# Dummy products in TensorE's wait for x, two small loads held back, and a new planned order, in a fused attention and state-space kernel

## The chip, the cores and the metric

One core of one Trainium2 chip runs the whole kernel as one program. The metric is the device time of one execution in microseconds; each version's number is the median of its runs.

## The reference

x is 2048 tokens of 448 features, bf16. Two branches read the same x, and a gate mixes them.

```python
x = A_x                                              # (1, 2048, 448)
g = sigmoid((x * gate_w).sum(-1, keepdims=True))
# A: attention, 16 heads of 28, one K and one V head for all
q = (x @ wq) as 16 heads;  k = x @ wk;  v = x @ wv
a = softmax(q k^T * 28**-0.5) v, heads joined, @ wo
# B: state-space convolution, 448 channels, 256 modes
dt = exp(log_dt);  logdA = dt * (A_re + i A_im);  dB = dt * (B_re + i B_im)
K[d, l] = Re sum_n C[d, n] exp(logdA[d, n] * l) dB[d, n]
b = causal convolution of x with K, over l, + x * Dskip
return g * a + (1 - g) * b
```

## The kernel before

Nobody writes the instruction order by hand. The kernel registers operations (`pg.op` for an engine, `pg.dma` for a load or store), each with what it reads and writes, an estimated duration and a priority; the planner (`Prog.schedule`) then simulates the five engines and fixes one order per engine. Lower (time, priority, number) goes first. Until the first exponential is planned, an operation on a longer remaining path to it can pass another; `RANK` adds nanoseconds to that path for single operations, named by their number. `LOW` is the share of a 3,413 ns stretch that TensorE should be busy: where the plan shows less, `idle` puts filler products (L1423, into P·V's bank, adding zeros) into a planned gap. `AHEAD` and `SLACK` shift when the planner takes a bank or a dependent operation for ready.

**The start.** SP issues the loads of x in four blocks of 512 tokens, in the order `QO` = 0, 3, 1, 2. Blocks 0 and 3 arrive as they are and TensorE transposes them in four parts T each (L718), from banks 0 and 1, copied to SBUF by ScalarE where the pair (block, T) is in `XA` (L728) and by VectorE else (L730). Blocks 1 and 2 come transposed by the DMA (L153, on SP's queue). Then four products per block make K (L736; block 2 in bank 5), VectorE takes the largest absolute value (L742), and K's copy to SBUF is VectorE's where the block is in `KD` (L746), else ScalarE's (L750). The first head's query follows: four products (L954), a maximum (L960), the bias weights (L768, L774, L775), a product that adds the bound (L963), the copy (L966). After that the first scores (L1337) and the first exponential (L1372) can run. V's and the gate's weights are loaded from GpSimd's queue (L632, L633) and copied by VectorE (L645, L647) for V's products (L763). Dummy products (`self.warm`, L554) on the identity are placed at several points here; the identity comes from GpSimd (L541, L542). ScalarE also prepares the state-space parameters, with three changes of its function table (the last, to exp, at L911).

**The middle.** 1024 score tiles of 128 keys by 512 queries are taken in sets of three and two. TensorE makes scores with 4 row-tiled products (L1337) or one over masked queries (L1347), ScalarE takes the exponential (L1372), TensorE multiplies with V (L1409). Beside that VectorE builds 14 groups of tables of powers (L1029 to L1075), TensorE turns them into kernels (L1095), GpSimd writes these to DRAM, SP loads them back as Toeplitz tiles (L1131), and TensorE convolves (L1155).

**The end.** The last heads are divided by their sums (`norm_last`: L1244, L1247, L1248), multiplied with wo (`outp`, L1198; L1265), added to the output with the gate (`fold`, L1207), while the last convolutions are scaled (L1170), turned (L1181) and added (L1189); then the stores.

Of the kernel before, what the change touches and what calls it, by code (L numbers as in the profile page):

```python
# [35 lines left out]
TW = 4 * 1024  # L36
XQ = NT * 512
SIN2PI = 6.2831850
XA = ((0, 1), (0, 3), (1, 0), (1, 1), (1, 2), (2, 3), (3, 0), (3, 1), (3, 2))
KD = (0, 2, 3)  # L40
GX = 3
DQ = (1, 2)
VNS = 140
# [41 lines left out]
class Prog:  # L85
# [6 lines left out]
    BLOCK, FIRST, FETCH, IDLE, NEED = 256, 192, 5900.0, 3300.0, .015  # L92
    HALF = (21000.0, 21000.0, 1.8)
    HEAD = 0.4
    RANK = {111: 3000, 190: -6000, 29: -6000, 38: -6000, 43: 3000, 23: -1500, 41: -3000, 192: -6000, 82: -1500, 153: -6000, 27: -3000, 118: 1500, 37: 1500, 150: -6000, 105: 3000, 39: -6000, 74: -1500, 92: 3000}
    POOL = (7,)
    LOW, SPAN, FILL = .45, 3413.0, (36000.0, 490000.0)
    AHEAD = 1500.0
    SLACK = {"pe": 700.0, "dve": 150.0}

    def __init__(self, nc, es):
        self.nc, self.es = nc, es
# [356 lines left out]
class Kernel:  # L459
# [131 lines left out]
    def loads(self):  # L591
# [37 lines left out]
        pg.dma(rows(wst, 0, ins["A_wq"], D), (448, 896), "wq", wr=["wqs"], cost=1500, extra=300)  # L629
        lx(QO[2])  # L630
        lx(QO[3])
        pg.dma(rows(wks, 4 * DH, ins["A_wv"], DH), (448, 56), "wv", wr=["wvs"], eng="pool", cost=150, extra=2500)  # L632
        pg.dma([(wks.v(0, P, 8 * DH, [[2, 3]]), dram(ins["gate_w"], 0, [[1, P], [P, 3]])),  # L633
                (wks.v(0, 64, 8 * DH + 6, [[1, 1]]), dram(ins["gate_w"], 384, [[1, 64], [1, 1]]))], (448, 2), "wg", wr=["wgs"], slow=True, eng="pool", cost=150, extra=2500)
# [67 lines left out]
    def prep_x(self):  # L702
        pg = self.pg
# [3 lines left out]
        for iq, q in enumerate(QO):  # L707
            xT, xo = self.xq(q)
            t4, o4 = self.bank((4, 3, 2, 5)[iq])
            X = ("b", (4, 3, 2, 5)[iq])  # L710
            for T in (2, 0, 3, 1) if q not in DQ else ():
                b = nb % 2
                nb += 1
                t, o = self.bank(b)

                def mm(e, q=q, T=T, t=t, o=o):
                    for k in range(4):
                        r = e.matmul(t.v(0, P, o + 128 * k, [[1, 128]]), xst.v(0, P, q * XP + k * D + 128 * T, [[1, P]]),  # L718
                                     self.ident.v(0, P, 0, [[1, P]]), start=True, stop=True, tile_position=(0, 0),
                                     skip_group_check=True)  # L720
                    return r
                pg.op("pe", mm, 415, rd=[("xst", q), "id"] + ["xp"] * (T == 3), wr=[("b", b)])
                last = len(pg.ops) - 1
                src = bass.AP(tensor=t.h, offset=o, ap=[[t.rs, P], [128, 4], [1, 2], [2, 64]])
                dst = xT.v(0, P, xo + T * 512, [[128, 4], [64, 2], [1, 64]])
                key = ("xT", T, q)
                if (q, T) in XA:
                    pg.op("act", lambda e, d=dst, s=src: e.activation(d, s, AF.Copy), 535, rd=[("b", b)], wr=[key])  # L728
                else:
                    pg.op("dve", lambda e, d=dst, s=src: e.tensor_copy(d, s), 600, rd=[("b", b)], wr=[key])  # L730

            for _ in range((2, 0, 0, 0)[iq]):
                pg.after[len(pg.ops)] = last
                self.warm(1, 5, 300)
            for n, T in enumerate((2, 0, 3, 1)):
                pg.op("pe", lambda e, n=n, T=T, t4=t4, o4=o4, xT=xT, xo=xo: e.matmul(  # L736
                    t4.v(0, P, o4, [[1, 512]]), self.Wk.v(0, P, T * P, [[1, P]]), xT.v(0, P, xo + T * 512, [[1, 512]]),
                    start=(n == 0), stop=(n == 3), tile_position=(0, 0), skip_group_check=True),
                    215, rd=["Wk", ("xT", T, q)], wr=[X])
                self.k3 = len(pg.ops) - 1  # L740
            kv, od = kT.v(0, P, 512 * q, [[1, 512]]), [[1, 512]]
            pg.op("dve", lambda e, q=iq, t4=t4, o4=o4: e.tensor_reduce(  # L742
                sm.v(0, P, 8 + q, [[1, 1]]), t4.v(0, P, o4, [[1, 512]]), AX.X, ALU.max, apply_absolute_value=True), 600,
                rd=[X], wr=[("km", iq)])
            if q in KD:
                pg.op("dve", lambda e, kv=kv, t4=t4, o4=o4, od=od: e.tensor_scalar(  # L746
                    kv, t4.v(0, P, o4, od), sm.v(0, P, 0, [[1, 1]]), None, ALU.add), 600,
                    rd=[X, "s0"], wr=[("kT", q)], pr=-2)
            else:
                pg.op("act", lambda e, kv=kv, t4=t4, o4=o4, od=od: e.activation(  # L750
                    kv, t4.v(0, P, o4, od), AF.Identity, bias=sm.v(0, P, 0, [[1, 1]])), 580,
                    rd=[X, "s0", ("km", iq)], wr=[("kT", q)], pr=-2)
            if q:
                o = pg.dma([(dram(self.XS, (q - 1) * P * XQ + o, [[XQ, n], [1, w]]), xT.v(0, n, xo + o, [[1, w]]))
                            for o, n, w in ((0, P, 1536), (1536, 64, 512))],
                       (128, 4096), f"xs{q}", rd=self.xk(q), wr=[("XS", q)], pr=0.3)
                self.lastxs = o.i
# [380 lines left out]
    def conv(self, c):  # L1138
# [29 lines left out]
        if c % 8 == 7 and c < 24:  # L1168
# [1 line left out]
        pg.op("dve", lambda e: e.tensor_tensor(self.cst.v(0, P, cs * 512, [[128, 4], [64, 2], [1, 64]]),  # L1170
                                               ps.v(0, P, 63, [[128, 4], [64, 2], [-1, 64]]),
                                               self.omq.v(0, P, 0, [[0, 4], [64, 2], [1, 64]]), ALU.mult),
              el(512), rd=[X, "omq"], wr=[("cst", cs), X], pr=(2, 2)[c > 25])
        Y = ("yx", c)

        def yt(e, k):
# [7 lines left out]
                                 start=(mu == 0), stop=(mu == 1), tile_position=(0, 64 * par), skip_group_check=True)  # L1184
            return r
        for k in range(4):
            pg.op("pe", lambda e, k=k: yt(e, k), 70, mode="h", ni=8, rd=[("cst", cs), "id"], wr=[Y], pr=1.55)
        ov = self.O.v(0, P, 15 * D + 16 * c, [[-D, 16], [1, 16]])
        pg.op("dve", lambda e: e.tensor_tensor(ov, ov, px.v(0, P, 0, [[1, 16], [16, 16]]), ALU.add),  # L1189
              el(256), rd=[Y], comm=tuple(("O" if c < 26 else "Oz", q) for q in range(7)), pr=(2, 0.5)[c > 25], unlock=px)  # L1190
# [1 line left out]
    def outp(self, qc, tt):  # L1192
        pg = self.pg
        X = ("ox", qc, tt)
        G = self.grp()
        px = lambda: G.v(0, P, 0, [[1, D]])
        for g in range(4):
            pg.op("pe", lambda e, g=g: e.matmul(  # L1198
                px(), self.onT.v(0, P, g * 512 + 128 * tt, [[1, 128]]), self.Wo.v(0, P, g * D, [[1, D]]),
                start=(g == 0), stop=(g == 3), tile_position=(0, 0), skip_group_check=True), 200,  # L1200
                rd=["Wo"] + [("on", gg) for gg in (0, 1, 2, 4 if (qc, tt) == (3, 2) else 3)], wr=[X], pr=1.2 if qc == 3 else 1.65, lock=G if g == 0 else None)
        self.fold(qc, tt, px, 0, D, [X], unlock=G)

    def fold(self, qc, tt, px, off, n, rd, unlock=None):
        tl = 4 * qc + tt
        ov = self.O.v(0, P, D * tl + off, [[1, n]])
        self.pg.op("dve", lambda e: e.scalar_tensor_tensor(ov, px(), self.gt.v(0, P, tl, [[1, 1]]), ov, ALU.mult, ALU.add),  # L1207
                   el(n), rd=rd + ["gt"], comm=(("O", qc + tt * (qc == 3)), ("Oz", qc + tt * (qc == 3))), pr=(2, 1.5)[qc == 3], unlock=unlock)

    def norm(self, i):  # L1210
        pg = self.pg
# [20 lines left out]
    def norm_last(self, i, o, n, bank, key):  # L1232
# [2 lines left out]
        hv, rv, on = w(self.acc, 512 * (i % 2)), w(self.rdenB, 0), w(self.onT, 512 * (i % 4))  # L1235
        ak = [("acc", i % 2, o) if o else ("acc", i % 2)]
        if bank is None:
            G, pe, dve = self.grp(), 0.9, 0.9
            bc, bk = lambda: G.v(0, P, 0, [[1, n]]), [("bx", i, o)]
        else:  # L1240
            G, pe, dve = None, 0, 0
# [45 lines left out]
    def main(self):  # L1287
# [36 lines left out]
        def qk(s):  # L1324
# [4 lines left out]
            def row(e):  # L1329
                for t, b in zip(ts, bs):  # L1330
                    if joint(t):
                        full(e, t, b, 1)
                for j in range(4):
                    for t, b in zip(ts, bs):
                        i, parts, qo, n = dec(t)
# [168 lines left out]
```

## Time and profile before

| what | value |
|---|---|
| runs, us | 504.24, 505.18, 506.43 (median 505.18) |
| profiled execution, us | 505.32 |
| its span, us | 503.5 |
| ScalarE busy | 480.7 us (95%) |
| VectorE busy | 456.9 us (91%) |
| TensorE busy (matmul) | 427.1 us (85%) |
| GpSimd busy | 169.7 us (34%) |
| DMA moved | 139.51 MB |

The span runs from the program's first to its last instruction; the execution's time adds what lies around it. Profile times are microseconds from the span's start. PE is TensorE's matmul part, PEld its weight loads, DVE is VectorE, ACT ScalarE, POOL GpSimd, and a "q" behind a name (SPq) stands for the sequencer that issues. In a line on a group of instructions, the numbers behind the bar are busy time and mean ns of one, then the idle time of the engine just ahead of them and what ended it. The granted clock is the share of TensorE's clock that the chip let through.

### The profile page before, as it was taken

Reading aid. Unit: us, or ns where it says so; the run is one execution under the profiler, and the core shown is the slowest. Engines: PE = TensorE matmul, PEld = TensorE weight load, DVE = VectorE, ACT = ScalarE, POOL = GpSimd, SP = SyncE. Lnnn points to the kernel's source line nnn. Section 1 sums busy time; section 2 is a strip of 40 time slices with the busy share of each in tenths; the row PEclk is TensorE's granted clock in tenths of the full one; section 3 lists DMA queues with packets and bytes.
Section 4 is the critical chain, followed back from the end, with each engine's and each line's share of the span. In section 5 each row is a group of like instructions: output and inputs, shape, how many; then the busy total and the mean of one; then the engine's idle time right before and its main releaser. Section 6 shows DMA issues by size and latency. Waiting matters only on the chain.

```text
span 503.5 us, 18673 instructions
## 1 busy us (share of the span) xinstructions
PE 427.1 (85%) x8288; PEld 190.9 (38%) x8395; DVE 456.9 (91%) x836; ACT 480.7 (95%) x430; POOL 169.7 (34%) x312
## 2 busy tenths in 40 slices
PE   5887878787797899779888899889888899899985
PEld 2322123242343434334443444344444444343543
DVE  7999999999999999999999999999999999923333
ACT  5899899999999999999999999999999999999971
POOL 8833223432143423414344421535042252514000
PEclk9899799999999999999999999999999999999989
DMA  8976921899959696999999989799997979799992
GB/s 189 218 209 124 60 35 44 280 292 350 328 186 306 225 349 211 285 367 329 354 318 364 336 303 366 210 357 378 356 364 249 369 256 387 242 347 365 385 343 47
DMA packets 122563, 139.51 MB, mean 277 GB/s; under 512 B 55321, under 2 KB 62538, under 8 KB 122482
## 3 DMA queue, kind: packets, MB, share of 16 engines
q1 hardware_dynamic: 112208, 128.89, 79.9%
q0 software_dynamic: 8784, 9.27, 6.9%
q8 instruction: 66, 1.08, 0.9%
q10 hardware_dynamic: 1490, 0.14, 0.2%
q14 instruction: 15, 0.12, 0.1%
HBM read 125.18 MB, written 5.22 MB: 259 GB/s over the span
## 4 chain that ended last, share of the span: by engine, by line
DVE 44%; ACT 42%; PE 10%; SPq 2%; issue 1%; DMA 1%; DVEq 0%
ACT expT L1372 42%; DVE tab L1048 7%; DVE tab L1059 4%; DVE tab L1060 4%; DVE tab L1070 3%; DVE tab L1057 3%; DVE tab L1058 3%; DVE msq L991 3%; DVE tmp L1066 2%; PE psS L1347 2%; DVE seedz L993 2%; DVE cst L1170 2%; DVE mbf L1011 2%; DVE seedz L995 1%; PE psB L1409 1%; PE psS L1337 1%
## 5 line engine op out<-in xcount | busy, mean ns | idle before, releaser
L1372 ACT ACTIVATE expT<-psS 128x1536 bf16<-128x1536 f32 (+1 forms) x410 | 465.6, 1362 | 7.1 <-PE psS L1337 4.6
L1347 PE MATMUL psS<-qM,kT 128*128 128x512 bf16 x310 | 103.0, 389 | 30.1 <-ACT expT L1372 17.5
L1409 PE MATMUL psB<-expT,vaug 128*32 128x512 bf16 (+2 forms) x1152 | 104.6, 367 | 1.8 <-DVE acc L1229 1.2
L1337 PE MATMUL psS<-qT,kT 29*128 29x512 bf16 (+2 forms) x690 | 82.9, 365 | 25.7 <-ACT expT L1372 22.1
L154 POOL DMA_DIRECT2D KP_scratch<-kstg x112 | 61.3, 556 | 66.3 <-DVE mbf L1011 30.6
L1048 DVE TENSOR_TENSOR tab<-tab,mbf 128x512 bf16<-128x512 bf16 (+3 forms) x56 | 64.6, 1154 | 0.0
L1409 PEld LDWEIGHTS psB<-expT,vaug 128*32 128x32 bf16 x1152 | 29.0, 93 | 79.4 <-issue 74.8
L154 POOL DMA_DIRECT2D rdenB<-R_scratch x56 | 29.1, 525 | 68.3 <-DMA R_scratch<-denT 66.0
L1337 PEld LDWEIGHTS psS<-qT,kT 29*128 29x128 bf16 x690 | 21.5, 91 | 70.1 <-ACT expT L1372 53.8
L1347 PEld LDWEIGHTS psS<-qM,kT 128*128 128x128 bf16 x404 | 25.4, 98 | 49.2 <-ACT expT L1372 35.5
L154 POOL DMA_DIRECT2D qM<-qT x64 | 32.8, 521 | 31.8 <-DVE seedz L995 12.6
L1059 DVE TENSOR_TENSOR tab<-tab 128x128 bf16<-128x128 bf16 (+4 forms) x70 | 41.8, 597 | 0.0
L1060 DVE TENSOR_TENSOR tab<-tab 128x128 bf16<-128x128 bf16 (+4 forms) x70 | 41.7, 596 | 0.0
L1155 PE MATMUL psX<-T,U 128*32 128x128 bf16 (+7 forms) x1408 | 34.1, 220 | 0.6 <-DMA T<-KP_scratch 0.2
L1070 DVE TENSOR_TENSOR tab<-tab,tmp 128x4096 bf16<-128x4096 bf16 x14 | 32.0, 2286 | 0.1
L1057 DVE TENSOR_TENSOR tab<-tab,mbf 128x4096 bf16<-128x4096 bf16 x14 | 32.0, 2288 | 0.0
L1155 PE MATMUL psS<-T,U 128*20 128x128 bf16 (+7 forms) x1312 | 31.6, 220 | 0.5 <-DVE qT L966 0.2
L1058 DVE TENSOR_TENSOR tab<-tab,mbf 128x4096 bf16<-128x4096 bf16 x14 | 31.9, 2281 | 0.0
L1095 PE MATMUL psS<-tab 128*32 128x64 bf16 x1280 | 30.1, 242 | 0.2
L1155 PEld LDWEIGHTS psX<-T,U 128*32 128x32 bf16 (+7 forms) x1408 | 24.6, 94 | 14.6 <-issue 9.9
L154 POOL DMA_DIRECT2D denT<-acc x14 | 10.0, 718 | 54.5 <-DVE acc L1229 50.7
L991 DVE TENSOR_TENSOR msq<-seedz 128x384 f32<-128x384 f32 (+1 forms) x50 | 27.6, 552 | 0.1
(163 smaller groups left out, 536.7 us busy)
## 6 DMA issues: line engine op xcount, KB each, us to landing
T<-KP_scratch SPq DMA_DIRECT2D x170, 512.0 KB, 8.2
U<-KP_scratch SPq DMA_DIRECT2D x40, 512.0 KB, 9.5
tab<-KP_scratch SPq DMA_DIRECT2D x14, 512.0 KB, 10.6
rdenB<-R_scratch POOLq DMA_DIRECT2D x56, 64.0 KB, 5.5
qM<-qT POOLq DMA_DIRECT2D x64, 32.0 KB, 4.9
tab<-in_A_x_dram SPq DMA_DIRECT2D x8, 224.0 KB, 3.8
O<-cst SPq DMA_DIRECT2D x1, 1792.0 KB, 11.8
KP_scratch<-kstg POOLq DMA_DIRECT2D x112, 16.0 KB, 4.4
```

The lines of the kernel that those rows point to most:

```text
L154: return [e.dma_start(o, i, **kw) for o, i in pairs]
L1048: vo(lambda e, dst=dst, src=src, mri=mri: e.tensor_tensor(dst, src, mri, ALU.mult), 4 * n, done + mk(lv), [kr, ki, tk])
L1057: vo(lambda e, src=src, mi=mi, tv=tv: e.tensor_tensor(tv, src, mi, ALU.mult), 2 * n, done + mk(lv), [tk])
L1058: vo(lambda e, dst=dst, src=src, mr=mr: e.tensor_tensor(dst, src, mr, ALU.mult), 2 * n, done + mk(lv), [kr, ki, ("gap", s)])
L1059: vo(lambda e, dc=dc, tc=tc: e.tensor_tensor(dc[0], dc[0], tc[1], ALU.subtract), n, [tk, kr], [kr])
L1060: vo(lambda e, dc=dc, tc=tc: e.tensor_tensor(dc[1], dc[1], tc[0], ALU.add), n, [tk, ki], [ki])
L1070: vo(lambda e: e.tensor_tensor(tab.v(0, P, FM, [[4, 1024], [1, 4]]), tab.v(0, P, lo + 124, [[CG, 32], [-4, 32], [1, 4]]), rho.v(0, P, 0, [ ...
L1155: r = e.matmul(ps.v(32 * j, 32 - 2 * n, 128 * k, [[1, 128]]), self.U.v(0, P, (4 * gi + j) * 32 + 2 * n, [[1, 32 - 2 * n]]), tbuf.v(0, P, t ...
L1337: r = e.matmul(self.psS.v(0, P, 512 * b + o, [[1, n]]), kT.v(32 * h, DH + 1, 128 * kt, [[1, 128]]), qT.v(32 * h, DH + 1, 512 * (i % 2) + q ...
L1347: r = e.matmul(self.psS.v(0, P, 512 * b, [[1, 512]]), kT.v(0, P, 128 * kt, [[1, 128]]), self.qM.v(0, P, (i % 2) * XQ + 512 * h + qo, [[512 ...
L1372: pg.op("act", lambda e: e.activation(expT.v(0, P, 512 * es[0], spread(es, n)), self.psS.v(0, P, 512 * bs[0], spread(bs, n)), AF.Exp, scal ...
L1409: r = e.matmul(self.psB.v(32 * h, 32, qo, [[1, n]]), vaug.v(0, P, 32 * kt, [[1, 32]]), expT.v(0, P, o, [[1, n]]), start=(h, kt) in first[v ...
```

## The change

- Block 3 (the second in `QO`) gets eight more dummy products into bank 5, registered as not before its transposes; each is one 128x512 product on the identity. All later operations' numbers rise by 8, and `RANK` names other operations.
- The loads of V's weights and of the gate's weights wait for block 0's first transpose (T = 2).
- `XA` and `KD`: the copy of (block 0, T = 0) and K's copies of blocks 0 and 2 go from VectorE to ScalarE. (Pairs of blocks 1 and 2 in `XA` have no effect.)
- `LOW` from .45 to .53, `AHEAD` from 1500 to 3000, VectorE's `SLACK` from 150 to 300.
- Priorities of the last stage: for convolutions past the 25th the scaling 1 for 2; turns 1.3 for 1.55; out products of the last quarter 0.9 for 1.2, their `fold` 1 for 1.5; `norm_last` without a bank of its own 1.5 and 2 for 0.9 and 0.9.
- In `qk`, the last product of a joint tile is kept as the one that signals.

```diff
-XA = ((0, 1), (0, 3), (1, 0), (1, 1), (1, 2), (2, 3), (3, 0), (3, 1), (3, 2))
-KD = (0, 2, 3)
+XA = ((0, 0), (0, 1), (0, 3), (1, 0), (1, 2), (1, 3), (2, 0), (2, 1), (2, 2), (3, 0), (3, 1), (3, 2))
+KD = (3,)
...
-    RANK = {111: 3000, 190: -6000, 29: -6000, 38: -6000, 43: 3000, 23: -1500, 41: -3000, 192: -6000, 82: -1500, 153: -6000, 27: -3000, 118: 1500, 37: 1500, 150: -6000, 105: 3000, 39: -6000, 74: -1500, 92: 3000}
+    RANK = {198: -6000, 29: -6000, 38: -6000, 41: -3000, 200: -3000, 82: -1500, 27: -1500, 126: 6000, 105: 3000, 39: -6000, 201: 6000, 20: -1500, 18: -6000, 17: -3000, 47: -3000, 81: -3000, 45: 3000, 121: 3000, 86: 3000, 64: -6000, 160: -3000, 46: -700}
     POOL = (7,)
-    LOW, SPAN, FILL = .45, 3413.0, (36000.0, 490000.0)
-    AHEAD = 1500.0
-    SLACK = {"pe": 700.0, "dve": 150.0}
+    LOW, SPAN, FILL = .53, 3413.0, (36000.0, 490000.0)
+    AHEAD = 3000.0
+    SLACK = {"pe": 700.0, "dve": 300.0}
...
         lx(QO[3])
+        self.late = [len(pg.ops), len(pg.ops) + 1]
         pg.dma(rows(wks, 4 * DH, ins["A_wv"], DH), (448, 56), "wv", wr=["wvs"], eng="pool", cost=150, extra=2500)
...
                 last = len(pg.ops) - 1
+                if iq == 0 and T == 2:
+                    for i in self.late:
+                        pg.after[i] = last
...
                 self.warm(1, 5, 300)
+            for _ in range(8 * (iq == 1)):
+                pg.after[len(pg.ops)] = last
+                self.warm(1, 5, 218, 0.6)
...
-              el(512), rd=[X, "omq"], wr=[("cst", cs), X], pr=(2, 2)[c > 25])
+              el(512), rd=[X, "omq"], wr=[("cst", cs), X], pr=(2, 1)[c > 25])
...
-            pg.op("pe", lambda e, k=k: yt(e, k), 70, mode="h", ni=8, rd=[("cst", cs), "id"], wr=[Y], pr=1.55)
+            pg.op("pe", lambda e, k=k: yt(e, k), 70, mode="h", ni=8, rd=[("cst", cs), "id"], wr=[Y], pr=1.3)
...
-                rd=["Wo"] + [("on", gg) for gg in (0, 1, 2, 4 if (qc, tt) == (3, 2) else 3)], wr=[X], pr=1.2 if qc == 3 else 1.65, lock=G if g == 0 else None)
+                rd=["Wo"] + [("on", gg) for gg in (0, 1, 2, 4 if (qc, tt) == (3, 2) else 3)], wr=[X], pr=0.9 if qc == 3 else 1.65, lock=G if g == 0 else None)
...
-                   el(n), rd=rd + ["gt"], comm=(("O", qc + tt * (qc == 3)), ("Oz", qc + tt * (qc == 3))), pr=(2, 1.5)[qc == 3], unlock=unlock)
+                   el(n), rd=rd + ["gt"], comm=(("O", qc + tt * (qc == 3)), ("Oz", qc + tt * (qc == 3))), pr=(2, 1)[qc == 3], unlock=unlock)
...
-            G, pe, dve = self.grp(), 0.9, 0.9
+            G, pe, dve = self.grp(), 1.5, 2
...
-                        full(e, t, b, 1)
+                        r = full(e, t, b, 1)
```

## The prediction

> **What bounds the kernel now.** First the page's head, then the two engines over the middle and over the end (groups of instructions, ScalarE alone).
>
> ```profile
> span 503.5 us, 18673 instructions
> PEclk9899799999999999999999999999999999999989
> L1372 ACT ACTIVATE expT<-psS 128x1536 bf16<-128x1536 f32 (+1 forms) x301 | 341.7, 1377 | 0.2
> L1372 ACT ACTIVATE expT<-psS 128x1536 bf16<-128x1536 f32 (+2 forms) x44 | 50.4, 1278 | 3.3 <-PE psS L1337 2.6 <-PE psS L1347 0.5
> ```
>
> The third line is 100 to 440 us, the fourth 440 to 503 us. From 100 to 440 ScalarE's exponentials idle 0.2 us in 340. So the end is: start of the first exponential, plus 465.6 us of them (page), plus ScalarE's idle time, plus a tail. The last ends at 489.08 + 4.25 = 493.3, the tail is 10.2 us. Idle before exponentials is 7.1 us in all (page): 2.05 before the first, 0.93 + 0.48 near 57 to 60 us, 3.3 after 440. A change can win at those places and nowhere else. VectorE is 99.8% busy in the same stretch (339.17 of 340), but it runs beside ScalarE, not ahead of it.
>
> Then the chain of waits up to the first exponential, read as start, duration, what:
>
> ```profile
> 8.91 4.65 DMA T<-in_A_x_dram
> 14.21 1.20 PE psS L736 x3
> 15.64 1.48 PE psS L736 x3
> 17.12 0.72 PE psX L954 x2
> 17.84 0.86 PE psS L736 x4
> 18.92 0.86 PE psS L554 x4
> 20.04 0.69 DVE qT L960
> 21.05 0.39 PE psX L963
> 22.74 5.97 ACT expT L1372 x5
> ```
>
> TensorE waits for the transposed x until 13.60 and then runs K's products. Last, stretches of 3.41 us, laid on the profile's own clock steps (stretch, length, busy and count of PE, PEld, DVE, ACT, POOL, granted clock, DMA share, GB/s):
>
> ```profile
> 10.75:14.16 3.41, 0.56 (x6) 0.43 (x7) 3.34 (x3) 3.41 (x6) 3.27 (x3) 1.00 1.10 203
> 14.16:17.58 3.42, 3.20 (x9) 1.18 (x8) 2.78 (x6) 3.36 (x4) 3.11 (x6) 0.50 1.05 201
> ...
> 31.23:34.64 3.41, 2.06 (x18) 0.70 (x17) 3.28 (x9) 3.41 (x4) 0.00 (x0) 1.00 0.38 80
> ...
> 51.71:55.12 3.41, 1.83 (x13) 0.51 (x13) 3.41 (x14) 3.41 (x4) 0.00 (x0) 1.00 0.76 54
> 55.12:58.54 3.42, 3.06 (x15) 0.64 (x16) 3.42 (x12) 2.49 (x3) 2.65 (x5) 0.50 0.91 50
> ```
>
> After a stretch with 0.56 or 1.83 us of TensorE work the next one runs at half clock; after 2.06 it doesn't. The same again at the end: 1.80 us in 478.37 to 481.78, then 0.50.
>
> **The change, part by part.** (a) **Dummies and the clock.** Before: TensorE stands 3.16 us, to 13.60. Eight products at the full-clock pitch of 0.216 (four L554 take 1.03 from 18.76, the last 0.38: 0.65 / 3) are 1.73 us; they fit, so they cost nothing. If the x landed before them they would cost up to 1.73, but bank 5, which they write, is next used by the block that lands last (16.3). They fill 10.3 to 12.0, so the stretch 10.75 to 14.16 gets 1.3 more: 1.9, between 1.83 (lost) and 2.06 (kept). What it buys if kept: eight products between 14.36 and 17.68 run 0.43 apart (two L736 from 16.07, the next pair at 16.92) and would run 0.216 apart, 1.7 us. But block 2 cannot start before its own landing: second issue at 10.83 + 1.35 = 12.18, 4.1 us to landing, 16.3. So its four products move from 17.68 to 16.35, 1.33. Behind them the query's products and four dummies (18.76 to 19.62) held L960 to 20.04; with all Q products done before 16.3, VectorE follows directly: last K product ends 17.38, L742 0.69, L775 0.34, L963 0.39, L966 0.68, L1337 0.44, with 0.05 to 0.1 between: first exponential possible at 20.25, 2.5 us earlier.
>
> [...]
>
> (b) **Copies moved to ScalarE.** One x copy (block 0, part 0: 0.60) and K's copies of blocks 0 and 2 (0.67 each, row L750) come to ScalarE, off VectorE (0.68 and twice 0.74; its relief counts nothing, as it is not ahead of ScalarE). ScalarE has no idle time from 7.87 until its exp table is in (19.40 + 1.28 = 20.68). The x copy falls into the 1.42 us it waits before 7.87. K's copies add 1.34: 22.0 with nothing else, so ScalarE, not TensorE, sets the new start.
>
> (c) **The held loads.** GpSimd issues V's and the gate's loads from 1.42 and 3.36, 2.8 us in all, and its identity (L542) comes at 2.97 because of the first. Without them the identity is ready near 1.5; today its dummies hold the first transpose (landing 5.43 for the block, by 1.64 + 3.8) to 6.02. So the transposes can start 0 to 0.6 earlier, I take 0.4. Dummies from 1.5 also fall into the stretch 0.51 to 3.92, which held 0.60 us of work before the clock came up at 7.34; if it comes up earlier, the first eight transposes run 0.06 apart (four from 7.44 in 0.40) and not 0.107 (eight from 6.02 in 1.06): 0.4 more. ScalarE's chain starts with them: 22.0 - 0.8 = 21.2. Block 2's copy may fall among the exponentials, which costs the same. Queued behind the two issues on GpSimd (now some 6 to 9 us) are K's weight copy (L637, 6.63; if it lands behind, block 0's products slip 2.8, still before 13.6) and U's copies, first needed by a transfer issued at 46 us. The loads land by 9 + 3.8 = 12.8; V's products start at 23.04: covered by 10 us. SP's queue keeps its issues. So the first exponential moves by 0.5 (ScalarE at 22.0, and 0.2 for the next product) to 2.5 (TensorE's path); I take 22.74 - 21.2, **-1.5**.
>
> [...]
>
> (d) **LOW .45 to .53**: more fillers in P.V where the plan shows TensorE idle. One filler (0.216) lifts 1.83 to 2.05, next to the 2.06 that kept the clock. The half clock from 55.12 to 61.95 cost 0.93 + 0.48 = 1.4 of ScalarE. Bounds -1.4 and 0; I take **-1.4**. A filler costs nothing while it lies in TensorE's waits for exponentials (27 us before scores from 100 to 440: 14.7 and 12.6 in the waits).
>
> (e) **Tail and order** (priorities of out products, norm, last convolutions; AHEAD, SLACK, RANK). In the middle there is 0.2 us to win. At the end, 100 convolution products take 1.61 (from 495.86) before the last copy, multiply and store; in the 2.3 us from 494.99 to 497.29, where the last norm waits on VectorE, TensorE has place for them already. Ends: -1.6 if they go ahead, +1.6 if they go behind the out products; I take **-0.3**.
>
> Sum: 505.32 (the profiled execution; span 503.5, 1.8 around it) - 1.5 - 1.4 - 0.3 = **502.1**. The median of the runs shown is 505.18, 0.14 lower, which I leave out.
>
> **The rivals.** *A, more of it*: the late idle time goes too. Of the 3.3 us after 440, 1.33 is a gap in TensorE's issue at 478.74 and the next is the half clock it sets off at 481.79; another order moves both. 2.3 more is 505.32 - 1.5 - 1.4 - 2.6 = 499.8. For: that gap is waited for by nothing the profile shows. Against: TensorE is 31.15 of 34 busy there. *B, ScalarE bounds the start*: K's copies eat the gain, start -0.5, rest as above: 503.1. For: no idle on ScalarE from 7.87. *C, the dummies don't hold the clock*: 1.9 falls below the step; the start gains only the first 0.4 of (c), 503.2. [...] *D, slower*: fillers stand ahead of scores. ScalarE has 0.2 us of slack in 340, so each filler that delays a scores group costs 0.216. Raising LOW by .08 asks for at most 0.27 us a window, 1.3 fillers; 133 windows, up to 170 fillers. Fourteen delayed groups eat the 2.9 us of start and clock; 25 give 505.32 - 2.9 + 5.4 = 507.8. Against: the 27 us of waits, and only 21 fillers in the trace of before.
>
> **How the numbers follow.** Forecast 0.47, A 0.22, B 0.08, C 0.10, D 0.13. Forecast's own range is 500.8 to 502.9. A measurement of this kernel can tell about 0.5%, 2.5 us: faster is below 502.65. Six in seven of the forecast (0.40) and A make faster 0.62; the rest of it with B and C 0.25; D 0.13. The range 499.0 to 505.5 holds all but D and the lower part of A.
>
> **What would show it.** (a): clock 1.00 from 14 to 17.6 and L736 products 0.216 apart; wrong if 0.50 stands there. (b): the exp table in, and the first exponential, near 21. (c): L542 near 1.5, first transposes by 5.7. (d): no 0.50 near 55 us, more L1423. (e): last exponential to end under 10.2. Wrong altogether if idle time before exponentials from 100 to 440 rises above 2 us.

## The result and the profile after

| | before | changed |
|---|---|---|
| median, us | 505.18 (504.24 to 506.43, 6 runs) | 510.31 (508.80 to 513.19, 6 runs) |
| ratio | | 1.0113, 95% interval 1.0079 to 1.0146 |
| profiled execution, us | 505.32 | 510.27 |
| its span, us | 503.5 | 508.3 |

The change made the kernel 1.1% slower; 502.1 was predicted. From the page of the changed kernel: span, granted clock in 40 slices, the queue that carries instructions (packets, MB, share of 16 DMA engines), and the exponentials (busy, mean ns | idle time before them). Lines here are those of the changed file: L1379 was L1372, L1344 was L1337, L1354 was L1347, L743 was L736, L757 was L750.

```profile
span 508.3 us, 18733 instructions
...
PEclk9898899999999999998999999999999999999999
...
q8 instruction: 66, 1.08, 0.9%
...
L1379 ACT ACTIVATE expT<-psS 128x1536 bf16<-128x1536 f32 (+1 forms) x410 | 465.9, 1350 | 10.1 <-PE psS L1344 6.1
```

ScalarE alone, in 22 to 100, 100 to 440 and 440 to 510 us of the changed kernel:

```profile
L1379 ACT ACTIVATE expT<-psS 128x1536 bf16<-128x1536 f32 x65 | 74.5, 1354 | 4.3 <-PE psS L1344 2.3 <-PE psS L1354 2.0
...
L1379 ACT ACTIVATE expT<-psS 128x1024 bf16<-128x1024 f32 (+1 forms) x298 | 338.5, 1365 | 3.5 <-PE psS L1354 1.6 <-PE psS L1344 1.6
...
L1379 ACT ACTIVATE expT<-psS 128x1536 bf16<-128x1536 f32 (+2 forms) x50 | 57.0, 1263 | 2.5 <-PE psS L1344 2.3
```

The last number but the releasers is what to read: from 100 to 440 us it was 0.2 before and is 3.5 now. Put together as the prediction did (start, exponentials, idle time, tail), in us:

| part | before | after | difference |
|---|---|---|---|
| first exponential starts | 22.74 | 23.71 | +1.0 |
| exponentials, busy | 465.6 | 465.9 | +0.3 |
| ScalarE's other work among them | 0.2 | 0.9 | +0.7 |
| idle, first exponential to 100 us | 1.4 | 2.7 | +1.3 |
| idle, 100 to 440 us | 0.2 | 3.5 | +3.3 |
| idle, past 440 us | 3.3 | 2.5 | -0.8 |
| last exponential to the end | 10.2 | 9.6 | -0.6 |

That is 5.2 for a span longer by 4.8; the parts are rounded and neighbouring exponentials overlap (410 of 1.350 us on average are 553.5 us, and ScalarE is busy with them for 465.9).

**The start.** The chain of waits (start, duration, what), then ScalarE's timeline of the same stretch (in brackets the idle time before and who ended it):

```profile
8.91 5.96 DMA T<-in_A_x_dram
...
15.53 2.39 PE psS L743 x7
17.92 0.85 PE psX L961 x2
18.77 1.25 PE psS L743 x4
20.02 0.86 PE psS L554 x4
...
21.35 0.70 DVE qT L967
```

```profile
20.84 1.28 ACT L918 ACT_TABLE_LOAD   x1
23.71 1.45 ACT L1379 ACTIVATE expT<-psS 128x1536 bf16<-128x1536 f32 x1 [1.59 <-PE psS L1344]
25.06 0.68 ACT L757 ACTIVATE kT<-psS,small 128x512 bf16<-128x512 f32 x1
```

The transposed x takes 5.96 us from its issue where it took 4.65, and lands at 14.87 for 13.55. The exp table is in at 22.12 (20.69 before), later, not earlier. K's copy of block 2 stands among the exponentials: 0.68. The clock, in two of its stretches (stretch, length, busy of PE, PEld, DVE, ACT, POOL, granted clock, DMA share, GB/s):

```profile
12.61:16.01 3.40, 0.87 (x7) 0.63 (x9) 2.29 (x3) 2.71 (x4) 3.03 (x7) 1.00 1.29 214
16.01:19.43 3.42, 3.42 (x10) 1.22 (x9) 2.89 (x6) 3.36 (x5) 2.94 (x8) 0.50 0.81 171
```

The eight dummies ran from 10.00 to 11.9, and TensorE stood for 3.04 us, up to 15.14. They fell into the stretch before; the one just ahead of the half clock kept 0.87 us of work. K's four products of block 2 take 1.46 us from 18.56, the larger part of it at half clock (to 19.4); before they took 1.03 from 17.68, just behind the half clock.

**Two stops.** TensorE alone, then all engines, from the changed kernel's timeline:

```profile
44.48 1.10 PE L837 MATMUL psS<-acc,onT 16*128 16x64 f32 x8 [1.15 <-DVE acc L831]
45.73 0.38 PE L1354 MATMUL psS<-qM,kT 128*128 128x512 bf16 x1 [0.16 <-issue]
```

```profile
229.15 0.24 PE L1162 MATMUL psX<-T,U 128*30 128x128 bf16 x4
...
231.16 1.04 PE L1354 MATMUL psS<-qM,kT 128*128 128x512 bf16 x2 [1.77 <-ACT expT L1379]
...
232.23 1.02 ACT L1379 ACTIVATE expT<-psS 128x1024 bf16<-128x1024 f32 x1 [1.20 <-PE psS L1354]
```

At 44.48 the gate's products stand ahead of scores and wait for VectorE; ScalarE loses 1.34 at 46.15, and the clock is half from 46.7 to 53.6. At 229.39 TensorE stops for 1.77 us. The profile names an exponential as releaser, but the one whose bank these scores need had ended at 229.69, 1.5 us earlier. What fits is a packet of the instruction queue (q8): begun at 228.72, landed at 229.88. The half clock follows at 231.1 to 234.5, and ScalarE loses 2.1 us there. The second stop is 1.37 us at 288.57; a packet had landed at 288.46.

The counts of instructions say the same. The changed kernel's trace has 8,426 weight loads on TensorE; with a product for each and 61 waits and drains that makes 16,913 instructions, and over the 66 packets of 16 KB 256 for each. Counted in this way from the start, the two stops stand at 6,083 and 8,388, 3 and 4 instructions behind 192 plus a multiple of 256. I call these places block edges. Of the 63 stops over 0.8 us between 100 and 440 us in the 20 profiled executions of this case, 62 stand 1 to 4 instructions behind a block edge.

The planner knows these edges, which the section on the kernel before leaves out: `BLOCK, FIRST, FETCH, IDLE = 256, 192, 5900.0, 3300.0`. It takes a block for loaded 5.9 us after TensorE has passed the edge before (3.3 us where it holds the DMA queue for empty), and lets operations of low priority wait so that an edge isn't reached early. Both versions have the same numbers. In the changed kernel TensorE ran through the blocks ahead of the two stops in 5.5 and 6.0 us, but could go on only 7.4 us after the edge before, later than the 5.9 that the plan allows. Why these two packets came late is not shown.

### The profile page after: what moved, and what is told of

It reads as the page before. It is cut to its first block, busy times and chain, and to the rows that moved or that the text cites. A ratio compares the mean times of both kernels' runs of the same rounds, so it can differ in the third digit from the quotient of the medians.

```text
span 508.3 us, 18733 instructions
## 1 busy us (share of the span) xinstructions
PE 435.0 (86%) x8319; PEld 194.8 (38%) x8426; DVE 456.1 (90%) x833; ACT 483.0 (95%) x433; POOL 164.8 (32%) x312
## 3 DMA queue, kind: packets, MB, share of 16 engines
q8 instruction: 66, 1.08, 0.9%
## 4 chain that ended last, share of the span: by engine, by line
ACT 78%; PE 12%; DVE 5%; issue 2%; SPq 2%; DMA 1%
ACT expT L1379 78%; PE psS L1354 2%; PE psB L1416 2%; PE psS L1344 2%; DMA T<-in_A_x_dram 1%; PE psS L1162 1%; SPq L153 1%; SPq L154 1%; PE psS L743 1%; DVE T L895 1%; PE psX L1205 1%; DVE msq L998 0%; PE psX L1251 0%; DVE seedw L895 0%; PE psX L961 0%
## 5 line engine op out<-in xcount | busy, mean ns | idle before, releaser
L1379 ACT ACTIVATE expT<-psS 128x1536 bf16<-128x1536 f32 (+1 forms) x410 | 465.9, 1350 | 10.1 <-PE psS L1344 6.1
L1354 PE MATMUL psS<-qM,kT 128*128 128x512 bf16 x317 | 104.0, 387 | 29.2 <-ACT expT L1379 16.8
L1344 PE MATMUL psS<-qT,kT 29*128 29x512 bf16 (+2 forms) x690 | 83.9, 365 | 26.3 <-ACT expT L1379 22.7
L1344 PEld LDWEIGHTS psS<-qT,kT 29*128 29x128 bf16 x690 | 21.6, 91 | 71.5 <-ACT expT L1379 56.7
L1354 PEld LDWEIGHTS psS<-qM,kT 128*128 128x128 bf16 x404 | 25.4, 98 | 46.5 <-ACT expT L1379 30.9
L1067 DVE TENSOR_TENSOR tab<-tab 128x128 bf16<-128x128 bf16 (+4 forms) x70 | 41.8, 597 | 0.0
L1066 DVE TENSOR_TENSOR tab<-tab 128x1024 bf16<-128x1024 bf16 (+4 forms) x70 | 41.7, 597 | 0.0
L1162 PE MATMUL psX<-T,U 128*32 128x128 bf16 (+7 forms) x1440 | 33.0, 220 | 0.0
L1162 PE MATMUL psS<-T,U 128*18 128x128 bf16 (+7 forms) x1280 | 31.3, 220 | 0.0
L1162 PEld LDWEIGHTS psS<-T,U 128*18 128x18 bf16 (+7 forms) x1280 | 21.8, 93 | 12.7 <-issue 9.4
```

The source lines that it names most:

```text
L1066: vo(lambda e, dc=dc, tc=tc: e.tensor_tensor(dc[0], dc[0], tc[1], ALU.subtract), n, [tk, kr], [kr])
L1067: vo(lambda e, dc=dc, tc=tc: e.tensor_tensor(dc[1], dc[1], tc[0], ALU.add), n, [tk, ki], [ki])
L1162: r = e.matmul(ps.v(32 * j, 32 - 2 * n, 128 * k, [[1, 128]]), self.U.v(0, P, (4 * gi + j) * 32 + 2 * n, [[1, 32 - 2 * n]]), tbuf.v(0, P, t ...
L1344: r = e.matmul(self.psS.v(0, P, 512 * b + o, [[1, n]]), kT.v(32 * h, DH + 1, 128 * kt, [[1, 128]]), qT.v(32 * h, DH + 1, 512 * (i % 2) + q ...
L1354: r = e.matmul(self.psS.v(0, P, 512 * b, [[1, 512]]), kT.v(0, P, 128 * kt, [[1, 128]]), self.qM.v(0, P, (i % 2) * XQ + 512 * h + qo, [[512 ...
L1379: pg.op("act", lambda e: e.activation(expT.v(0, P, 512 * es[0], spread(es, n)), self.psS.v(0, P, 512 * bs[0], spread(bs, n)), AF.Exp, scal ...
```

## The experiments

Times are medians. Ratios are against the kernel before on the same chip; they are estimated from all runs and can differ by 0.3% from the quotient of the medians. Runs on different chips are compared by their ratios.

**The planner runs again after each edit of the source, and an edit can move operations everywhere.** The first four undo or do one part each in the source.

Without the hold of the two loads:

```diff
-                if iq == 0 and T == 2:
-                    for i in self.late:
-                        pg.after[i] = last
```

> The changed kernel, with the loads of V's and the gate's weights issued at once again; all else as changed. In the profile of the changed kernel the transposed block 1 lands at 14.87 us, before at 13.55, and the first exponential starts at 23.71, before at 22.74. Theory H (the held loads, small as they are, run beside the transposing transfer and push it back): block 1 lands near 13.6 again, the first exponential comes by 22.5 and the time falls by 1.0 to 2.0 us, to 508.5 to 509.5. Theory S (block 1's landing scatters between executions, the hold does nothing): block 1 still lands after 14.3 or the first exponential does not move, and the time stays within 0.7 us of 510.3.

Measured: 515.67 us, ratio 1.0192 (1.0137 to 1.0247). Block 1 lands at 12.84, as theory H said, but the new order puts GpSimd's copy of K's weights at 14.34, and the first exponential starts at 26.13. The time tells of that order, not of the hold.

The new start with the old numbers and priorities:

```diff
-    LOW, SPAN, FILL = .53, 3413.0, (36000.0, 490000.0)
-    AHEAD = 3000.0
+    LOW, SPAN, FILL = .45, 3413.0, (36000.0, 490000.0)
+    AHEAD = 1500.0
...
```

> The changed kernel's start (dummies, hold, copies, RANK) with LOW .45, AHEAD 1500, SLACK 150 and the priorities of the last stage as before. ScalarE lost 8.5 us before exponentials after the first one in the changed kernel, 5.05 before. Theory K (the numbers in the planner, fillers above all, cost the 3.5 us): the time falls by 2.5 to 4 us, to 506.3 to 507.8, and the idle time before exponentials after the first falls to 5 to 6 us. Theory F (the start costs it all, by what it pushes into the later order): the time stays within 1 us of 510.3.

Measured: 512.42, ratio 1.0123 (1.0076 to 1.0171); idle 100 to 440: 5.3 us. Theory K falls: the idle time after the first exponential is 11 us, not 5 to 6. By its ratio the time is that of the changed kernel, as theory F said. So idle time in the middle comes without the new settings too.

The old start with the new numbers and priorities (the same diff the other way round, on the kernel before):

> The kernel before with only LOW .53, AHEAD 3000, SLACK 300 and the new priorities of the last stage; its start is the old one. Theory K: slower than before by 2.5 to 4 us, 507.7 to 509.2. Theory F: within 1 us of 505.2. The forecast (fillers keep the clock up, the tail is shorter) would have 503.0 to 504.0.

Measured: 512.77, ratio 1.0144 (1.0091 to 1.0196). The start is good (first exponential 21.42, no half clock there), the middle nearly so (1.0 us idle); one gap of 8.19 us at 474 in the new order's last stage eats it. None of the three forecasts has this time. Neither half alone brings the time back: each plan loses somewhere else.

The hold alone, on the kernel before:

> The kernel before with only the two loads held back to block 0's first transpose. Theory H: block 1 lands at 14.5 to 15.0 in place of 13.55 and the first exponential comes 0.8 to 1.5 us later than 22.74; time 506.0 to 506.7. Theory S: block 1 lands at 13.5 to 13.8, first exponential at 22.74 or earlier by up to 0.5, time 504.7 to 505.2.

Measured: 508.04, ratio 1.0036 (1.0012 to 1.0060). Block 1 lands at 14.13, the first exponential starts at 23.78; ScalarE's idle time after it (5.0) and the tail (10.14) stay. This is theory H by itself: 1.0 us in the profiled start, though block 1 lands a little earlier than it said and the ratio gives 1.8 us (0.6 to 3.0). The planner hardly moved anything here: of TensorE's order only 13 of the first 73 places differ from the kernel before's, and none behind them.

**From here on every order is kept.** The finished order is edited behind the planner: `move` puts operations behind another on one engine, `reclock` counts the semaphore waits anew.

```diff
             self.pg.schedule()
+            self.pg.move("pool", (57, 58), 81)
+            self.pg.reclock()
```

> The changed kernel with every engine's order kept, but for GpSimd's queue: the loads of V's and the gate's weights stand behind the fourth copy into U instead of the first (issue near 12.3 us instead of 7.5). Theory H (these loads, moved beside x's transposed transfer, make it land late): block 1 lands near 13.5 us instead of 14.87, the first exponential starts 1.0 to 1.4 us earlier (22.3 to 22.7), and the time is some 1.2 us under the changed kernel's (about 509, ratio near 1.009). Rival (the order, not the loads, sets the landing or the first exponential): landing within 0.4 us of 14.87 or first exponential still near 23.7, ratio near 1.011.

Measured: 509.32, ratio 1.0076 (1.0047 to 1.0104). Landing 13.10, first exponential 22.20, 1.5 us earlier than in the changed kernel. The place of the loads is shown in the profile; by the ratios the time lies 0.4%, some 1.9 us, under the changed kernel's, with intervals that overlap. Over all 20 profiled executions of both kernels and their variants, block 1 lands at 14.47 us on average where the loads are issued beside it (9 executions, 13.89 to 15.21) and at 13.43 where not (11, 12.84 to 13.99).

The same with eight more dummies behind the eight (`extra` issues so many products of so many columns behind an operation):

```diff
+            pg.extra = {113: (8, 512)}
```

> The same, and eight more dummy products behind the eight, order kept. Theory C (the half clock from 16.0 to 19.4 us comes because the eight dummies end 3 us before x is there): with products until about 13.6 us and x by then, no half clock before 22 us, block 2's products at 0.22 instead of 0.43 us each, the first exponential near 21.2 to 21.6, time about 507.7 (ratio near 1.006). Rival (the clock drops whatever runs in the gap, or VectorE and ScalarE set the first exponential): half clock between 13 and 20 us again, or first exponential within 0.3 us of f1's; ratio as f1's.

Measured: 510.91, ratio 1.0108 (1.0072 to 1.0145). Half of theory C holds: no half clock before 43.5 us, products 0.216 apart. But the first exponential stays at 22.23. ScalarE from 14 to 23.5 us of this run:

```profile
L1408 ACT ACTIVATE expT<-psS 128x1536 bf16<-128x1536 f32 x1 | 1.5, 1451 | 0.0
L786 ACT ACTIVATE kT<-psS,small 128x512 bf16<-128x512 f32 x2 | 1.4, 688 | 0.6 <-DVE small L778 0.5
L932 ACT ACT_TABLE_LOAD x1 | 1.3, 1283 | 0.0
L947 ACT ACT_TABLE_LOAD x1 | 1.3, 1283 | 0.0
...
```

The first exponential waits 0.0: the table (L947) is in at 22.22, while the scores were there at 21.15. With the clock held and x early, ScalarE with its two copies of K and the 0.6 us before them sets the start. In executions of the old start with the clock held it is 21.42 (e4), 21.59 (i1 below), 21.60 and 21.70 (the shifts by 64 and 128 below), and 22.50 where block 2 landed late, at 17.39 (by 192). The new start at its best is later than the old one at its best.

Only the places of TensorE's instruction fetches shifted, by 64 one-column products in the wait for x:

```diff
+            pg.extra = {113: (64, 1)}
```

> The changed kernel with its order kept and 64 one-column products (128 TensorE instructions) behind the eight dummies, where TensorE waits anyway until x lands. They shift the places in the program at which TensorE fetches its next 16 KB of instructions. Theory F (the stops of 1.77 us at 229.4 and 1.37 us at 288.6 us are waits for such a fetch): both are gone from there, the half clock at 231 us with them, and stops of 1.2 to 1.8 us, if any, stand elsewhere, each begun within 0.2 us of the end of a 16 KB packet; the time moves by the difference, between -3 and +2 us. Rival (they are waits for the exponentials that the order brings): both stay at their place within 0.1 us and 0.2 us in size, and the time is the changed kernel's within 0.7 us, ratio near 1.011.

Measured: 512.64, ratio 1.0137 (1.0107 to 1.0167). Theory F: the stop at 229 is gone, others stand elsewhere. The one at 288 is 0.87 for 1.37 at 286.6, so that place can't be called gone. By count both stand at the same block edge, which now lies 128 instructions earlier in the order. The stops here begin 0.1 to 0.7 us after a packet's landing, not all within the 0.2 that the theory gave. Idle 100 to 440 rises to 7.0, and by the ratios the time by 0.24%, 1.2 us.

The gate's products behind the next scores:

```diff
+            self.pg.move("pe", (227,), 291)
+            self.pg.reclock()
```

> The changed kernel with one step of TensorE's order changed: the gate's products, which wait for VectorE's copy, stand behind the next four score products instead of ahead of them. Theory G (scores queued behind the gate's products cost ScalarE the 1.34 us at 46.15 and bring on the half clock of 46.7 to 53.6): the gap of 1.34 us is under 0.3, no half clock within 44 to 54 us, idle after the first exponential falls from 8.5 by 1.5 to 2.2 us; time about 508.5, ratio near 1.008. Rival (the stretch is short of work for TensorE anyway and the clock falls with or without it): the half clock comes within 5 us of the same place, idle falls by less than 0.8, ratio near 1.011.

Measured: 509.49, ratio 1.0060 (1.0034 to 1.0085). Neither the 1.34 us nor a half clock near 46 to 54 is left, as theory G said. The idle time after the first exponential doesn't fall, though: in the profiled execution (510.56) more of it past 100 us (5.1 to 440) takes the gain back.

Both mends:

> The changed kernel, order kept but for both mends: the two loads behind the fourth copy into U, and the gate's products behind the next scores. If the parts add up (loads -0.4%, gate -0.5% against the changed kernel's 1.0113): ratio 1.001 to 1.005, block 1 landed by 13.5 us, first exponential 21.9 to 22.4, no gap over 0.5 us in 40 to 50 us. Rival (they overlap, the fetch stops eat the second gain): ratio 1.006 to 1.010.

Measured: 510.87, ratio 1.0104 (1.0061 to 1.0148). They don't add up. Landing 13.49 and no gap over 0.5 us in 40 to 50, as expected; the first exponential, at 22.52, is a little late after a half clock from 14.6 to 18.0. The stops at 226.5, 286.0 and 360.0 us (1.77, 1.40, 1.66) remain.

The fillers one column wide instead of 512:

```diff
-self.psB.v(0, P, 0, [[1, 512]]) ... vaug.v(0, P, 29, [[0, 512]])
+self.psB.v(0, P, 0, [[1, 1]]) ... vaug.v(0, P, 29, [[0, 1]])
```

> The changed kernel, order and instruction counts kept, with each of its fillers 1 column wide instead of 512, so that they take some 0.03 us instead of 0.216 and hold no clock. Theory N (fillers hold little and cost little; the loss lies in landing, fetches and the gate's place): ratio 1.009 to 1.014, half clock stretches between 36 and 62 us as many as in the changed kernel or one more. Rival D (fillers ahead of scores are the cost): ratio below 1.006 and idle after the first exponential 2 us or more below 8.5.

Measured: 513.70, ratio 1.0174 (1.0139 to 1.0208), mean clock 0.967 for 0.986, seven periods at half clock for three. The time is worse than theory N said, and rival D falls: the fillers hold the clock and cost less than they bring.

The dummies one column wide (`self.warm(1, 5, 218, 0.6)` with 1 column):

> The changed kernel, order and instruction counts kept, with the eight dummy products 1 column wide instead of 512, so that TensorE stands some 4.8 us instead of 3.0 before x is there. Step (a) of the prediction (they hold the clock) would make it 1.2 us or more slower: half clock from 13 to 18 us or longer, first exponential 24 us or later, ratio 1.013 or more. Rival (with x late and ScalarE's chain to 22.2 us they hold nothing that counts): first exponential 22.2 to 23.8 us, ratio 1.009 to 1.013.

Measured: 511.58, ratio 1.0136 (1.0106 to 1.0167). Half clock from 13.3 to 20.1, first exponential 24.25: half a us later than with full ones. Profile and ratio are as step (a) said, but the interval covers the rival's range too.

On the kernel before, eight dummies that stand at 17 and 19 us moved into the wait for x:

```diff
+            pg, early = self.pg, (144, 145, 146, 147, 158, 159, 160, 161)
...
+                pg.ops[m].deps, pg.ops[m].fn = {3: 1}, pg.ops[90].fn
+            pg.move("pe", early, 95)
+            pg.reclock()
```

The eight now wait for the identity alone and write bank 5; in the lines left out, operations that relied on their old waits take these over.

> The kernel before with its order kept, but for eight dummy products that it runs at 17 and 19 us anyway: they stand where TensorE waits for x to land, so that instruction counts behind them are unchanged. Theory C (dummies in that gap are worth what was predicted, where ScalarE has no more copies to make): no half clock at 14 us in the profiled execution, first exponential at 21.3 to 21.6 instead of 22.74, middle and end as before, profiled execution 1.0 to 1.5 us under before's, median ratio 0.996 to 1.000 (before has its half clock there not in every execution). Rival (the clock drops anyway, or comes back later without the two groups): half clock somewhere in 12 to 22 us, first exponential 22.3 or later, ratio 1.000 to 1.003.

Measured: 506.36, ratio 1.0031 (1.0007 to 1.0054). The half clock at 14 us is gone and back at 20.9 to 27.7, where the eight now lack. First exponential 21.78, but 1.15 us idle at 27 and 30 us, and 2.3 us in the middle (100 to 440), most of it at a stop at 340 us and the half clock behind it.

Also on the kernel before, two fillers from within its half clock put ahead of it:

```diff
+            f = self.pg.fill
+            f[319] = f.pop(332) + f.pop(336)
```

> The kernel before, order kept: the two fillers that stand at 56.9 and 58.5 us, within its half clock, stand at 52.9 us, ahead of it; instruction counts are the same from there on. Step (d) of the prediction (a filler or two lift the stretch of 1.83 us over the 2.06 that keeps the clock): no half clock within 50 to 62 us, the idle 0.93 + 0.48 us near 57 to 60 gone, the rest as before; profiled execution about 1.4 us under before's, median ratio 0.996 to 0.999. Rival (the clock's stretches lie elsewhere from run to run, so the half clock moves by some us and the cost stays): a half clock within 40 to 75 us again with 1 us or more of idle time there, ratio 0.999 to 1.002.

Measured: 504.95, ratio 1.0002 (0.9984 to 1.0021), profiled execution 503.90. Stretches of that execution:

```profile
51.20:54.60 3.40, 2.95 (x21) 0.80 (x19) 3.33 (x12) 3.40 (x5) 0.00 (x0) 1.00 0.76 54
54.60:58.00 3.40, 2.10 (x15) 0.43 (x11) 3.40 (x12) 3.40 (x4) 2.84 (x5) 1.00 0.99 51
```

At that place the step does what was predicted: clock 1.00 through, no idle time. But this execution has a half clock from 33.2 to 36.6 that the kernel before's doesn't have, with 0.57 us idle at 35, so the rival's half clock that moves is there as well, further away than it said. Of the 1.4 us by which the profiled execution lies under before's, 1.15 come from an earlier start (first exponential 21.59), which this edit doesn't touch. The median is level with the kernel before; no version here is faster.

**The order before, shifted.** The kernel before with the 64 one-column products behind operation 95:

> The kernel before with its order kept and 64 one-column products (128 TensorE instructions) put where TensorE waits for x to land, so that only the places of its instruction fetches shift. Theory F (before's order is fast in the middle because its fetches fall where TensorE has a pause; any plan that shifts them loses this): idle time before exponentials from 100 to 440 us rises from 0.2 to between 2 and 6 us, with stops of 0.8 to 1.8 us that begin at the end of a 16 KB packet, and the time is 507 to 511 us (ratio 1.004 to 1.012). Rival (the old order has slack for them, the new one is bad in itself): idle from 100 to 440 under 1 us, ratio 0.998 to 1.002.

Measured: 512.36, ratio 1.0152 (1.0112 to 1.0193). ScalarE from 100 to 440 us, and one of the stops on TensorE:

```profile
L1399 ACT ACTIVATE expT<-psS 128x1024 bf16<-128x1024 f32 (+1 forms) x296 | 336.2, 1373 | 6.1 <-PE psS L1364 5.7 <-PE psS L1374 0.2
```

```profile
194.96 0.70 PE L1122 MATMUL psS<-tab 128*32 128x64 bf16 x31
197.14 0.34 PE L1122 MATMUL psS<-tab 128*32 128x64 bf16 x9 [1.48 <-issue]
```

The stop falls within one group of 40 products, where no semaphore is waited for, hence "issue"; the instruction packet began at 194.52 and landed at 195.75, and TensorE stood still from 195.66. The planner doesn't count the added products, so all edges lie 128 instructions earlier in the order than it planned. Two more places for each order:

> The kernel before, order kept, shifted by 64 instructions. Theory F2: idle before exponentials from 100 to 440 us of 2 us or more, time 507 to 513 us, ratio 1.004 to 1.016. Rival W (the 128 of g1 was an unlucky place, the old order is good at most places): idle under 1 us there and ratio 0.998 to 1.003.

> The same with 192 instructions. Theory F2: ratio 1.004 to 1.016; Rival W: 0.998 to 1.003.

> The changed kernel, order kept, its fetches shifted by 64 instructions (32 one-column products where TensorE waits for x). Theory F2 (the order before owes its lead to where its fetches fall; at shifted places the two orders are alike): 508 to 514 us, ratio 1.006 to 1.018, the mean of the changed kernel's three shifts within 2 us of the mean of three shifts of the kernel before. Rival W (the changed order's own work is worse): its shifts stand 3 us or more above the shifts of the kernel before.

> The same with 192 instructions. Theory F2: 508 to 514 us; Rival W: as above, 3 us or more over the kernel before at the same shift.

| shift, instructions | before: ratio | idle 100 to 440 | changed: ratio | idle 100 to 440 |
|---|---|---|---|---|
| 0 | 1 | 0.2 | 1.0113 | 3.5 |
| 64 | 1.0172 (1.0109 to 1.0235) | 11.3 | 1.0191 (1.0110 to 1.0272) | 6.0 |
| 128 | 1.0152 (1.0112 to 1.0193) | 6.1 | 1.0137 (1.0107 to 1.0167) | 7.0 |
| 192 | 1.0128 (1.0063 to 1.0193) | 4.6 | 1.0105 (1.0059 to 1.0151) | 4.9 |
| mean of the shifted | 1.0151 | 7.3 | 1.0144 | 6.0 |

Idle times are those of one profiled execution. Theory F2 holds, with ratios a little over what it gave at two of the places for the old order and at one for the new: at shifted places the two orders are alike, medians 513.2 and 512.2 us on average, 1.0 apart. In the profiled executions of this table TensorE stops for more than 0.8 us 37 times between 100 and 440 us. Of these 36 begin as an instruction packet lands, within 0.7 us, and end 2.3 to 2.8 us after it began; all 37 stand 1 to 4 instructions behind a block edge. The kernel before has none in the middle.

A rival is that any disturbance costs the old order so much. Three runs keep the counts of the kernel before while its start changes: e5, g2 and i1 have 1.0, 2.3 and 0.9 us idle from 100 to 440, with none, one and one of these stops; the shifted orders have 4.6 to 11.3 us and 3 to 10 stops. So the places of the edges matter most. The shifts show what misplaced edges cost either order. They don't show that the old order met its edges by luck, since the planner had made room for them. A shift by a whole block of 256, which would put the edges back on their places, was not run.

## Why the prediction was wrong

Forecast 502.1, measured 510.3 (510.27 in the profiled execution).

**The step that failed** is (e): "In the middle there is 0.2 us to win", and middle 0 in the sum. It asked what could be won there and not what could be lost: against its sum 3.3 us were lost there, 2.5 in the start (c) and 2.7 between the start and 100 us (d). The 0.2 us was no property of the middle; it was a fit of one order to its block edges, made by the planner. Shifting these by 64 to 192 instructions, with the order kept, cost the kernel before 1.3 to 1.7%, more than the whole change does. The changed kernel has another order and another count of instructions, and in spite of the same planner two stops in the middle, with two more past 440 us (0.96 at 477.21, 1.27 at 483.10). Around the two in the middle ScalarE loses 2.1 and 0.4 us, most of the 3.3. The prediction set its own mark, 2 us of idle time from 100 to 440; it is 3.5. None of its rivals had this: D put the idle time down to fillers ahead of scores, and thin fillers made it worse.

Its own evidence had one such stop. The gap at 478.74 in the kernel before, which rival A calls "waited for by nothing the profile shows", fits a wait for instructions by the same signs:

```profile
480.06 0.27 PE L1337 MATMUL psS<-qT,kT 29*128 29x128 bf16 x4 [1.33 <-issue]
```

The packet began at 477.61 and landed at 478.70, and the stop stands 2 instructions behind a block edge. In e5, g2 and i1, where the counts are the same, it is there again with 1.33 us. Rival A counted it as idle time to win, and no rival asked whether a new order meets such waits elsewhere.

That a re-plan must lose there is not shown: the new settings on the old start (e4), with most of TensorE's order moved, have 1.0 us.

**(a) Dummies and the clock**, block 2's products from 17.68 to 16.35: not in the profiled execution (0.50 from 16.0 to 19.4; they start at 18.56). Whether the dummies hold the clock, single executions can't settle. For it: f2, with sixteen, has clock 1.00 up to 43.5 us and block 2's products from 16.27, and i3, with thin ones, loses the clock from 13.3. Against it: e4 and i1 keep the clock there with none in that gap. The step "between 1.83 (lost) and 2.06 (kept)" is no limit: in f5 a stretch with 1.75 us of TensorE work (13.58 to 17.00) was followed by clock 1.00, in i1 one with 2.29 (29.82 to 33.24) by 0.50. The stretches of 3.41 us themselves don't lie at the same times in every execution: the record of the granted clock begins at 7.34 us in the kernel before, at 9.19 in the changed kernel and at 10.17 in f5. With the same eight dummies, and x landing even later, at 15.21, f5 has no half clock there, and its first exponential starts at 22.54; in the changed kernel it is 23.71.

**(b) ScalarE at 22.0**: right, 22.12, and in f2 22.22. The prediction had the bound and then argued it away.

**(c) Held loads**: two mistakes. The transposes came as said (identity at 1.34, first transpose at 5.12), but "ScalarE's chain starts with them" was wrong: its first parameter activation comes right behind a copy of x (at 8.87), which had waited 0.68 us for TensorE, and starts at 9.36 for 9.45 before, so of the 0.8 us 0.1 is left. And the sum counts no price for the loads beside x, which is 1.3 us in the profiled pair (landing at 14.87 for 13.55) and 1.0 on average (14.47 for 13.43). The start, predicted at -1.5, is +1.0.

**(d) Fillers**, -1.4: that fillers hold the clock is borne out (g3, without them, has seven half clocks for three), the size is not to be had: the half clock of 55 us is at 46.7 now, behind the 1.15 us in which TensorE waits at the gate's products, and i1, with the one at 55 us gone but another at 33.2, has the median of the kernel before.

**(e) Tail**, -0.3: right in sign, -0.6.

What stays open: how the remainder divides. The single mends move the profile where they should, but each also moves half clocks and stops, and their medians don't add up.

## What to carry to other kernels

When an engine is 0.2 us from saturated over 340 us, ask first what keeps it there and what any re-plan may lose; a gain of 1 us at the start is small against that. To test one part of a change in a planned kernel, keep the finished order and edit only that part; thin a product to one column instead of taking it out, so that instruction counts stay. And where a planner counts instructions, an edit behind it that changes the count moves all block edges off their planned places (64 to 192 instructions cost the kernel before 1.3 to 1.7%): shift both orders before saying which one is better in itself.

## What the runs showed of the hardware

- The 66 packets of 16 KB on the queue q8 (1.08 MB) go with 16,913 TensorE instructions in the changed kernel's trace, 256 for each. Of the 37 stops over 0.8 us between 100 and 440 us in the table of shifts, 36 ended 2.3 to 2.8 us after an instruction packet had begun, and all stood 1 to 4 instructions behind 192 plus a multiple of 256. From the landing to the end of the stop it was 1.2 to 1.5 us (1.28 at 231.16 and 1.48 at 289.94 in the changed kernel, 1.36 at 480.06 in the kernel before). The profile names no releaser for such a stop ("issue", at 480.06 in the kernel before), or one that had ended 1.5 us earlier (an exponential, at 231.16 in the changed kernel).
- TensorE's busy time in a stretch of 3.41 us did not alone decide the clock of the next: 1.75 us were followed by 1.00 (f5), 2.29 by 0.50 (i1).
- Where four small loads (21, 3.5, 0.8 and 0.1 KB) were issued beside a transposed transfer of x, it landed 1.0 us later on average (14.47 in 9 executions, 13.43 in the 11 others). In the changed kernel these loads took 4.0 to 5.3 us themselves, for 3.5 to 3.8 in the kernel before.
